# Order and shape of the first loads: q weights in four row blocks ahead of most of x

## Chip, cores and metric

The kernel runs on one core of a Trainium2 chip. The metric is the time of one execution on the device in microseconds (us). Six runs of the kernel before gave 203.6 to 205.08, median 204.03.

## What is computed

Two branches share one layer norm and are added to the input:

```python
x = A_x                                   # (1, 2048, 512), bf16
xn = layernorm(x)
# A: sliding, dilated local attention: 32 heads of 16, window of 8 positions with a step of 2
q, k, v = split(xn @ wqkv)                # wqkv: (512, 1536)
logits = q . k[pos - 2 w] / 4, w = 0..7   # positions below 0 masked
A = (softmax(logits) . v[pos - 2 w]) @ wo
# B: gated MLP with a mix over positions
z = gelu(xn @ w_in)                       # w_in: (512, 1376)
z1, z2 = z[:, :688], layernorm(z[:, 688:])
B = (z1 * (w_sp @ z2 + b_sp)) @ w_out     # w_sp: (2048, 2048)
return x + A + B
```

## The kernel before, in words

**Tiles.** The 2048 rows of x are 16 tiles of 128 rows. Tile number i = 4 tb + j: tb (0 to 3) is a block of 512 neighbouring rows, j (0 to 3) the place in it. The work goes by j: "block j" is the four tiles 4 tb + j. All of x lies in one SBUF buffer, `xall` (in the profile `r_x`), the q and k weights in `wqk` (`r_w`), each as four row blocks of 128 input channels (kc = 0 to 3, since matmuls contract over 128 at a time).

**The path of a tile.** VectorE computes statistics of its 512 columns (`ln_stats`, L205 and L206, in one part or in two halves), ScalarE the square root (`ln_sqrt`, L209), VectorE the reciprocal and the normalization (`ln_recip`, L212; `ln_apply`, L216). Then the tile is transposed into `xnT`: tiles of block 0 and the first two of block 1 by TensorE (`tr`, L223) with ScalarE copying the result out of PSUM (`tr_copy`, L227), all others by a DMA transpose on SyncE's queue (`tr_dma`, L231). After that, `qk_part` (L308) multiplies by weights: `qk_part(pq, j, m, b0, b1)` makes, for block j, two of the four column groups of q (m = 0, 1) or of k (m = 2, 3), for the tiles tb = b0 to b1 - 1, with one matmul for each column group and row block kc. `qk_copy` (L318) casts the sums to bf16 with ScalarE.

**Order.** Nothing is scheduled by a planner: each engine works through its instructions in the order in which the program writes them, and waits on semaphores where data of others are needed. After the part shown below, a written list (`ORDER`, L42) fixes the rest: the products of the MLP, v, the logits, softmax, the mix over positions (L451), the output products and the stores.

**The loads** (L171 to L180). SyncE (SP) and ScalarE (A) each issue into a DMA queue of their own; both queues are served by the same 16 DMA engines. For block 0, tiles tb = 0 and 1 come as column halves, the left one on SP, the right one on A; tiles 2 and 3 follow as one transfer of 256 KB on A. On SP behind its two halves: the q weights in one transfer of 512 KB, block 1 of x, the k weights, blocks 2 and 3 of x, and half of `w_in`. ScalarE loads its function table behind its three DMAs.

**The start of the compute** (L557 on). TensorE runs ten warm-up matmuls while the first loads come in. VectorE normalizes tiles 0 and 1 of block 0 (statistics in two halves each, as they arrive), TensorE transposes them, two more warm-up matmuls follow, then come the q products m = 0 for tiles 0 and 1 (`qk_part(pqs[0], 0, 0, 0, 2)`, split in two by row blocks). Tiles 2 and 3 are normalized and transposed; between their transposes stand the products m = 1 for tiles 0 and 1. Then:

```python
    qk_part(pqs[0], 0, 0, 2, 3)          # q, m = 0, tile 2 alone
    qk_part(pqs[1], 0, 1, 2, 3)          # q, m = 1, tile 2 alone
    qk_part(pqs[2], 0, 2, 0, 2)          # first product with the k weights
    ...
    for n in range(2):
        qk_part(pqs[n], 0, n, 3, 4)      # q, tile 3 alone
        qk_copy(pqs[n], 0, n)
```

and the rest of block 0, block 1, and the list.

Of the kernel before, what the change touches and what calls it, by code (L numbers as in the profile page):

```python
# [15 lines left out]
P = 128  # L16
S = 2048
D = 512
NT = S // P
TB = 4  # L20
TBS = 512
C = D // P
# [48 lines left out]
def kernel(  # L71
# [14 lines left out]
    A = nc.scalar  # L86
    G = nc.gpsimd
    PE = nc.tensor
    SP = nc.sync

    x2 = A_x.rearrange("b s d -> (b s) d")
    out2 = out.rearrange("b s d -> (b s) d")
    xblk = x2.rearrange("(b j p) d -> j p b d", b=TB, j=4)
# [9 lines left out]
    xall = r_x[:, 0:4 * TB * D].rearrange("p (j b d) -> p j b d", j=4, b=TB)  # L103
    vp = r_x[:].rearrange("p (d t) -> p d t", d=DH)
    r_w = sb.tile([P, 8192], BF16, name="r_w")
    wqk = r_w[:, 0:4096].rearrange("p (s k f) -> p s k f", s=2, k=C)
# [54 lines left out]
    k_casts = [[] for _ in range(4)]  # L161
    k_reads = [[] for _ in range(4)]

    def load_x0(E, tb, h):
        E.dma_start(xall[:, 0, tb, 256 * h:256 * h + 256], x2[tb * TBS:tb * TBS + P, 256 * h:256 * h + 256])  # L165

    def load_wqk(E, s):
        E.dma_start(wqk[:, s],
                    A_wqkv[:, s * D:(s + 1) * D].rearrange("(k p) f -> p k f", p=P))

    for tb in range(2):  # L171
        load_x0(SP, tb, 0)
        load_x0(A, tb, 1)
    A.dma_start(xall[:, 0, 2:4, :], xblk[0][:, 2:4, :])
    load_wqk(SP, 0)
    SP.dma_start(xall[:, 1], xblk[1])
    load_wqk(SP, 1)
    for j in range(2, 4):
        SP.dma_start(xall[:, j], xblk[j])
# [21 lines left out]
    def ln_stats(i, parts=1):  # L201
        j, tb = i % 4, i // 4
        w = D // parts
        for h in range(parts):
            V.bn_stats(stats[:, i, 6 * h:6 * h + 6], xall[:, j, tb, w * h:w * h + w])  # L205
        V.bn_aggr(mv[:, i, :], stats[:, i, 0:6 * parts])  # L206

    def ln_sqrt(sl):
        A.activation(rstd[:, sl], mv[:, sl, 1], ACT.Sqrt, bias=eps_t[:])  # L209
# [92 lines left out]
    def qk_part(pq, j, m, b0, b1, ccs=(0, 1), p0=None, kcs=range(C)):  # L302
        sd, c0 = m // 2, 2 * (m % 2)
        p0 = b0 if p0 is None else p0
        xv = xnT[:].rearrange("p k (b j t) -> p k b j t", b=TB, j=4)
        for cc in ccs:
            for kc in kcs:
                PE.matmul(pq[:, cc, p0 * P:(p0 + b1 - b0) * P], wqk[:, sd, kc, c0 + cc:D:C],  # L308
                          xv[:, kc, b0:b1, j, :], start=(kc == 0), stop=(kc == C - 1))

    def qk_copy(pq, j, m, b0=0, b1=TB, p0=None):
        sd, c0 = m // 2, 2 * (m % 2)
        p0 = b0 if p0 is None else p0
        if sd == 0:
            dst = qs[:, j, c0:c0 + 2, b0 * P:b1 * P].rearrange("p c (b t) -> p c b t", b=b1 - b0)
        else:
            dst = ks[:, c0:c0 + 2, HALO:HALO + S].rearrange("p c (b j t) -> p c b j t", b=TB, j=4)[:, :, b0:b1, j, :]
        cast = A.copy(dst, pq[:, :, p0 * P:(p0 + b1 - b0) * P].rearrange("p c (b t) -> p c b t", b=b1 - b0))  # L318
        if sd == 1:
            for i in k_reads[j]:  # L320
                tc.declare_no_dep(cast.ins, i, reason="other token columns of the same rows")
            k_casts[j].append(cast.ins)

    def qk_tile():
        return ps_mm.tile([P, 2, TBS], F32, name="pq", tag="mm")
# [213 lines left out]
    def blk(j):  # L539
        return [4 * tb + j for tb in range(TB)]  # L540

    def col(i):
        return slice(i, i + 1)
# [13 lines left out]
    t0, i1 = blk(0), blk(1)  # L557
    i2, i3 = blk(2), blk(3)
    warm_up(10)
    for n in range(2):  # L560
        ln_stats(t0[n], 2)
        ln_sqrt(col(t0[n]))
    for n in range(2):
        ln_tile(t0[n])
# [11 lines left out]
    pqs = [qk_tile() for _ in range(3)]  # L576
# [3 lines left out]
    qk_part(pqs[1], 0, 1, 0, 2, (0,))  # L580
    tr_copy(t0[3], tr(t0[3]))
    qk_part(pqs[1], 0, 1, 0, 2, (1,))
    qk_part(pqs[0], 0, 0, 2, 3)
    qk_part(pqs[1], 0, 1, 2, 3)
    qk_part(pqs[2], 0, 2, 0, 2)
    for n in range(2):
        ln_stats(i1[n])
# [4 lines left out]
    ln_apply(i1[1])  # L592
    ln_stats(i1[3])
    for n in range(2):
        qk_part(pqs[n], 0, n, 3, 4)
        qk_copy(pqs[n], 0, n)
    ln_sqrt(slice(9, 16, 4))
    ln_stats(i2[0])
# [22 lines left out]
    pqs = [qk_tile() for _ in range(3)]  # L621
# [79 lines left out]
```

## Time and profile before

| what | value |
|---|---|
| median of six runs | 204.03 us |
| the profiled execution | 204.22 us |
| its span (first to last instruction) | 202.5 us |
| TensorE busy | 196.3 us, 97% of the span |
| VectorE busy | 187.1 us, 92% |
| ScalarE busy | 100.1 us, 49% |
| granted TensorE clock | 1.00 in all slices |
| DMA moved | 25.91 MB, 128 GB/s on the mean |

Start of the kernel in the timeline (us from the start of the span):

| engine | what | from | length |
|---|---|---|---|
| SP and A | two x halves each, issue | 0.81 | 0.87 and 0.90 |
| SP | q weights, issue | 1.73 | 0.43 |
| A | x tiles 2 and 3, issue | 1.74 | 0.46 |
| A | function table load | 2.22 | 1.28 |
| VectorE | statistics of tile 0, of tile 1 | 2.86, 3.78 | 0.75, 0.70 |
| TensorE | transposes of tiles 0 and 1 | 5.25, 5.77 | |
| TensorE | first q products | 7.17 | 1.06 |
| VectorE | statistics of tile 2, of tile 3 | 6.60, 7.42 | 0.69, 0.66 |
| TensorE | transposes of tile 2, of tile 3 | 8.86, 9.53 | 0.40, 0.39 |
| TensorE | 48 matmuls of 128 or 256 columns | 9.75 | 3.70 |
| VectorE | statistics of block 1 begin | 9.23 | |
| SP | first DMA transpose | 15.40 | 1.29 |

How to read the views that follow. The *chain of work* is followed back from the last instruction, at each step to what released it. A *wait* is idle time of an engine just before an instruction, with what ended it. In the table by stretches, each engine has its busy time and the number of its instructions, and the last three columns are the granted TensorE clock, the mean busy share of the 16 DMA engines (over 1 where packets overlap) and GB/s moved. PE is TensorE's matmul, PEld its weight load, DVE VectorE, ACT ScalarE, POOL GpSimd. Matmuls are pipelined, so the time from one start to the next says more than the duration of one.

### The profile page before, as it was taken

To read this page: it belongs to the slowest core of one execution; us is meant where nothing else is said; L and a number is where in the kernel's file an instruction comes from. 1 tells how busy PE (TensorE), PEld (TensorE's weight loads), DVE (VectorE), ACT (ScalarE), POOL (GpSimd) and SP (SyncE) were. 2 spreads that over 40 slices of the span, in tenths; PEclk is the share of its full clock that TensorE was granted. 3 is DMA by queue.
4 is the path that set the end of the run, shared out by engine and by line. 5 is a ranking of instruction groups with operands and counts; after the bars stand their busy time and mean duration, and the time that the engine had idled before them with its cause. 6 is when DMAs were issued, how large, how long until landed. Compare 5 with 4: busy or idle time off the path is not lost.

```text
span 202.5 us, 4070 instructions
## 1 busy us (share of the span) xinstructions
PE 196.3 (97%) x1687; PEld 124.6 (62%) x1691; DVE 187.1 (92%) x267; ACT 100.1 (49%) x162; POOL 11.7 (6%) x14
## 2 busy tenths in 40 slices
PE   7799999999999999999999999999999999999994
PEld 2599856555566666666556666666546645664562
DVE  5789899999999999999989998999999999999805
ACT  3466999999969984641742309647100210031000
POOL 3000000792000000000000000000000000000000
PEclk9999999999999999999999999999999999999999
DMA  5972558000397000695499966989717910744164
GB/s 149 359 256 53 104 103 238 10 0 3 71 181 165 3 0 0 120 258 114 33 231 206 177 163 105 207 166 189 163 40 195 212 43 0 223 95 94 51 200 136
DMA packets 66290, 25.91 MB, mean 128 GB/s; under 512 B 56224, under 2 KB 66016, under 8 KB 66016
## 3 DMA queue, kind: packets, MB, share of 16 engines
q1 hardware_dynamic: 65568, 25.19, 53.6%
q10 hardware_dynamic: 704, 0.47, 0.7%
q8 instruction: 13, 0.21, 0.4%
q14 instruction: 5, 0.04, 0.1%
HBM read 10.13 MB, written 2.10 MB: 60 GB/s over the span
## 4 chain that ended last, share of the span: by engine, by line
PE 93%; DMA 2%; DVE 2%; issue 1%; ACTq 0%; DVEq 0%
PE pg L451 37%; PE pz L237 19%; PE pq L308 13%; PE po L523 7%; PE pv L412 7%; PE po L499 6%; DMA r_x<-in_A_x_dram 2%; PE pl L362 1%; DVE r_qk L513 1%; PE po L508 1%; PE pb L499 1%; DVE stats L205 1%; PE pt L223 1%; PE pa L308 0%; ACTq L165 0%
## 5 line engine op out<-in xcount | busy, mean ns | idle before, releaser
L451 PE MATMUL pg<-z,r_qk 128*128 128x344 bf16 x448 | 67.3, 309 | 0.0
L451 PEld LDWEIGHTS <-r_qk 128*128 128x128 bf16 x448 | 43.7, 98 | 22.4 <-issue 0.8
L237 PE MATMUL pz<-w_z,xnT 128*128 128x344 bf16 x256 | 40.1, 309 | 0.0
L426 DVE TENSOR_TENSOR r_pr<-r_x,r_w 128x2048 bf16<-128x2048 bf16 x32 | 38.2, 1218 | 0.3
L430 DVE TENSOR_TENSOR r_pr<-r_pr 128x2048 bf16<-128x2048 bf16 x28 | 33.9, 1218 | 0.2
L457 ACT ACTIVATE gs<-pg,b_col 128x688 bf16<-128x688 f32 x16 | 13.3, 831 | 40.7 <-PE pg L451 25.1
L237 PEld LDWEIGHTS <-xnT 128*128 128x128 bf16 x256 | 24.9, 98 | 13.4 <-issue 0.8
L308 PE MATMUL pq<-xnT,r_w 128*128 128x256 bf16 (+2 forms) x192 | 28.8, 304 | 0.7 <-DMA r_w<-in_A_wqkv_dram 0.7
L342 DVE TENSOR_TENSOR r_pr<-r_qk 128x2048 bf16<-128x2048 bf16 x24 | 28.4, 1216 | 0.0
L308 PEld LDWEIGHTS <-r_w 128*128 128x128 bf16 x200 | 20.2, 114 | 7.8 <-DMA r_w<-in_A_wqkv_dram 1.1
L299 ACT ACTIVATE r_uz<-pz 128x688 bf16<-128x688 f32 x16 | 11.4, 741 | 22.5 <-PE pz L237 22.3
L318 ACT CAST r_qk<-pq 128x1024 bf16<-128x1024 f32 (+1 forms) x16 | 15.3, 990 | 2.4 <-PE pq L308 2.3
L523 PE MATMUL po<-r_w,r_uz 128*128 128x512 bf16 x66 | 14.9, 379 | 0.6 <-issue 0.6
L513 DVE TENSOR_TENSOR r_qk<-po,r_qk 128x512 bf16<-128x512 f32 x14 | 9.2, 686 | 6.0 <-PE po L523 6.0
L412 PE MATMUL pv<-xnT,r_w 128*32 128x512 bf16 x256 | 14.6, 380 | 0.0
L499 PE MATMUL po<-r_lg,r_pr 32*128 32x512 bf16 x224 | 14.5, 375 | 0.0
L523 PEld LDWEIGHTS <-r_uz 128*128 128x128 bf16 x85 | 8.0, 98 | 9.8 <-issue 1.5
L351 DVE TENSOR_TENSOR r_pr<-r_pr 128x4096 bf16<-128x4096 bf16 x6 | 13.7, 2283 | 0.0
L205 DVE BATCH_NORM_STATS2 stats<-r_x 128x6 f32<-128x512 bf16 (+1 forms) x18 | 10.8, 611 | 1.9 <-DMA r_x<-in_A_x_dram 1.9
L261 ACT ACTIVATE junk<-z 128x688 bf16<-128x688 bf16 x16 | 12.4, 778 | 0.2
L412 PEld LDWEIGHTS <-r_w 128*32 128x32 bf16 x256 | 9.4, 138 | 4.6 <-issue 0.3
L255 ACT ACTIVATE z<-pz 128x688 bf16<-128x688 f32 x16 | 11.8, 738 | 0.8 <-PE pz L237 0.8
(81 smaller groups left out, 175.1 us busy)
## 6 DMA issues: line engine op xcount, KB each, us to landing
r_lg<-in_A_wo_dram SPq DMA_DIRECT2D x8, 256.0 KB, 3.9
r_qk<-in_A_x_dram SPq DMA_DIRECT2D x16, 128.0 KB, 2.2
out_dram<-r_qk SPq DMA_DIRECT2D x15, 128.0 KB, 1.9
r_w<-in_A_wqkv_dram SPq DMA_DIRECT2D x3, 512.0 KB, 5.0
r_x<-in_A_x_dram SPq DMA_DIRECT2D x3, 512.0 KB, 6.4
w_z<-in_B_w_in_dram SPq DMA_DIRECT2D x2, 688.0 KB, 5.7
r_w<-in_B_w_out_dram SPq DMA_DIRECT2D x1, 640.0 KB, 4.8
r_x<-in_A_x_dram ACTq DMA_DIRECT2D x1, 256.0 KB, 4.8
```

The source lines that it names most:

```text
L237: PE.matmul(pz[:, hh, 0:FHALF], xnT[:, kc, i * P:(i + 1) * P], wz[:, kc, hh * FHALF:(hh + 1) * FHALF], start=(kc == 0), stop=(kc == C - 1))
L308: PE.matmul(pq[:, cc, p0 * P:(p0 + b1 - b0) * P], wqk[:, sd, kc, c0 + cc:D:C], xv[:, kc, b0:b1, j, :], start=(kc == 0), stop=(kc == C - 1))
L318: cast = A.copy(dst, pq[:, :, p0 * P:(p0 + b1 - b0) * P].rearrange("p c (b t) -> p c b t", b=b1 - b0))
L342: prod = V.tensor_tensor(pr[g % 3][:, c].rearrange("p w b t -> p b w t"), q3.unsqueeze(2).broadcast_to([P, TB, 4, P]), k4, ALU.mult)
L351: V.tensor_tensor(pr[g % 3][:, 0:2], pr[g % 3][:, 0:2], pr[g % 3][:, 2:4], ALU.add)
L412: PE.matmul(pv[32 * tb:32 * tb + 32, dd, :], wv[:, kc, 2 * d2 + dd, :], xnT[:, kc, tb * TBS:(tb + 1) * TBS], start=(kc == 0), stop=(kc == ...
L426: V.tensor_tensor(pw_t[n], vp[:, :, off:off + P], a_sb[:, slot_w(w), ts].unsqueeze(1).broadcast_to([P, DH, P]), ALU.mult)
L430: V.tensor_tensor(pw_t[n] if dst is None else dst, pw_t[n], pw_t[m], ALU.add)
L451: PE.matmul(pg[:, hh, 0:FHALF], wsp[n][:, k, :], z2[:, k, hh * FHALF:(hh + 1) * FHALF], start=(k == 0), stop=(k == NT - 1))
L457: A.activation(gs[:], tiles.pop(("g", n))[:, :, 0:FHALF], ACT.Identity, bias=b_col[:, i:i + 1])
L499: PE.matmul(pc, op[32 * tb:32 * tb + 32, d, o * P:(o + 1) * P], wo_r[32 * tb:32 * tb + 32, d, cs], start=(d == 8), stop=False, tile_positi ...
L523: PE.matmul(pc, uT[:, o % 2, m, tb * P:(tb + 1) * P], wout[:, m, cs], start=False, stop=(m == MCH - 3))
```

## The change

The left and right column halves remain for tile 0 only; tiles 1, 2 and 3 are each loaded whole on ScalarE's queue. SP issues its half of tile 0, then the q weights as four transfers of 128 input channels each, then what it issued before. The statistics of tile 1 are taken in one part. The q products for tile 2 alone and tile 3 alone become one call for both, at the place where tile 3's stood, so that the first product with the k weights moves ahead of them.

```diff
-    def load_x0(E, tb, h):
-        E.dma_start(xall[:, 0, tb, 256 * h:256 * h + 256], x2[tb * TBS:tb * TBS + P, 256 * h:256 * h + 256])
-
-    def load_wqk(E, s):
-        E.dma_start(wqk[:, s],
-                    A_wqkv[:, s * D:(s + 1) * D].rearrange("(k p) f -> p k f", p=P))
-
-    for tb in range(2):
-        load_x0(SP, tb, 0)
-        load_x0(A, tb, 1)
-    A.dma_start(xall[:, 0, 2:4, :], xblk[0][:, 2:4, :])
-    load_wqk(SP, 0)
+    def load_x0(E, tb, c0=0, c1=D):
+        E.dma_start(xall[:, 0, tb, c0:c1], x2[tb * TBS:tb * TBS + P, c0:c1])
+
+    def load_wqk(E, s, k0=0, k1=C):
+        E.dma_start(wqk[:, s, k0:k1],
+                    A_wqkv[:, s * D:(s + 1) * D].rearrange("(k p) f -> p k f", p=P)[:, k0:k1])
+
+    load_x0(SP, 0, 0, D // 2)
+    load_x0(A, 0, D // 2, D)
+    for tb in range(1, TB):
+        load_x0(A, tb)
+    for k in range(C):
+        load_wqk(SP, 0, k, k + 1)
     SP.dma_start(xall[:, 1], xblk[1])
     load_wqk(SP, 1)
...
     for n in range(2):
-        ln_stats(t0[n], 2)
+        ln_stats(t0[n], 2 - n)
         ln_sqrt(col(t0[n]))
...
     qk_part(pqs[1], 0, 1, 0, 2, (1,))
-    qk_part(pqs[0], 0, 0, 2, 3)
-    qk_part(pqs[1], 0, 1, 2, 3)
     qk_part(pqs[2], 0, 2, 0, 2)
...
     for n in range(2):
-        qk_part(pqs[n], 0, n, 3, 4)
+        qk_part(pqs[n], 0, n, 2, 4)
         qk_copy(pqs[n], 0, n)
```

## The prediction

> **What bounds the kernel now.** I read the page's chain of work first, then TensorE's waits, then the chain of the first 12 us, then the DMA traffic of those microseconds.
>
> ```profile
> PE 93%; DMA 2%; DVE 2%; issue 1%; ACTq 0%; DVEq 0%
> ```
>
> The chain that ended last is TensorE for 93% of the span. The 2% of DMA is one transfer at the start. The waits of TensorE over the whole span say the same:
>
> ```profile
> PE pwm L550 <- DVE warm L183: 1.1, 1, 1.1
> PE pq L308 <- DMA r_w<-in_A_wqkv_dram: 0.7, 1, 0.7
> PE po L523 <- issue: 0.6, 4, 0.2
> PE pt L223 <- DVE r_x L216: 0.6, 1, 0.6
> ```
>
> Columns: us in total, times, longest. After its start TensorE waits twice (0.68 us for the q weights at 7.17, 0.62 us for normalized x tile 2 at 8.86) and then never again by more than 0.16 us until the tail. So a microsecond won or lost before about 13 us arrives at the end one for one, as nothing behind it can absorb it or add to it. The chain through the second wait (start, length):
>
> ```profile
> 1.74 4.84 DMA r_x<-in_A_x_dram
> 6.58 0.02 issue
> 6.60 0.70 DVE stats L205
> ...
> 8.38 0.42 DVE r_x L216
> 8.81 0.05 issue
> 8.86 0.40 PE pt L223 x4
> ```
>
> x tiles 2 and 3 are one 256 KB transfer that lands 4.84 us after its issue; only then VectorE starts on them. VectorE had been idle since 5.71, so 0.89 us. Why the transfer is slow shows in a table by stretches (last two columns: DMA share, GB/s):
>
> ```profile
> 1.75:2.75 1.00, 1.00 (x4) 0.30 (x3) 0.07 (x1) 0.53 (x1) 0.81 (x4) 1.00 0.75 218
> 2.75:3.75 1.00, 1.00 (x4) 0.44 (x3) 0.85 (x3) 0.76 (x1) 0.00 (x0) 1.00 0.59 102
> 3.75:4.75 1.00, 1.00 (x4) 0.29 (x2) 0.96 (x5) 0.29 (x1) 0.00 (x0) 1.00 0.99 324
> 4.75:6.75 2.00, 1.56 (x12) 0.56 (x10) 1.05 (x4) 1.36 (x4) 0.00 (x0) 1.00 1.07 370
> 6.75:12.75 6.00, 4.96 (x63) 4.68 (x64) 5.72 (x18) 2.31 (x7) 0.00 (x0) 1.00 1.09 354
> ```
>
> There is a **trough**: the four small x transfers are through by about 3.0, and the next two (the 512 KB of q weights, the 256 KB of x), though issued at 1.73 and 1.74, hardly move before 3.75. That microsecond carries 0.10 MB where the later rate would carry 0.35 MB; 0.25 MB at 354 GB/s is **0.71 us lost**. From 3.75 on the DMA engines are full, so everything queued behind is late by it: the second x block (issue 2.20, 6.4 us to landing, so 8.6) and the k weights (512 KB more, 0.524/0.35 = 1.5 us later, so 10.1).
>
> **The change, part by part.**
>
> *Column halves of tile 1 and the pair of tiles 2 and 3 become three whole tiles on ScalarE's queue.* ScalarE issues four DMAs instead of three, 0.45 us each (rows of 0.40 to 0.47). Behind them in its queue stands the table load: 2.22 becomes 2.67, its 1.28 us end at 3.95. The first square root, now at 3.89, slips by 0.06; VectorE wants its result at 4.63, and the instruction takes 0.29, so 0.4 us of cover stays and I cost it at 0. Beyond that cover each 0.1 us would cost 0.1.
>
> *Statistics of tile 1 in one part.* Two halves took 0.70, one whole row of 512 takes 0.69 (tile 2's row): 0. But they now need all of tile 1 at 3.78, and the first tile's apply stands behind them on VectorE. Loads of this form (128 KB, one row per partition) exist in the trace, the residual x loads: 2.2 us to landing. From an issue at 1.24 that is 3.4, the lower bound. With what goes ahead of it (0.13 MB of 512-byte packets, then 0.26 MB at 354 GB/s, from 1.75) its last byte moves at about 2.9; the last of the 16 engines lands 0.5 to 0.8 behind (the old pair: some 5.9 by the same count, landed 6.58), so 3.4 to 3.7. If the whole trough falls ahead of it, 4.1 to 4.4, 0.3 to 0.6 too late. I take 3.7, nearest to the 2.2 us row: no cost.
>
> *Tiles 2 and 3.* By the same count tile 2 lands at 4.2 to 4.5, tile 3 (0.92 MB into the stream) at 4.9 to 5.2; even with the full trough under 6. Upper bound, the old 4.84 us from an issue at 2.2: 7.0. VectorE gets to them at 5.71 and 6.53. So VectorE's 0.89 us of idle go, and the chain to the transposes moves up whole: tile 2's from 8.86 to 7.97, tile 3's from 9.53 to 8.64. What is late next is VectorE itself, which is then without a gap: **0.89 us is the cap** of this part.
>
> *q weights in four row blocks.* SP issues 1 + 4 instead of 2 + 1 transfers ahead of the second x block. The build gives the fourth block a wait on the landing of tile 0's ScalarE half (3.04 now), as DMA semaphores are reused; queued behind on SP are the second x block (2.20 becomes 3.5), the k weights (2.75 becomes 4.0, behind tile 1's landing), and blocks 3 and 4 of x. As long as the rings hold data this is hidden: by 3.5 some 0.9 MB are queued, which last to 4.4. The first q products wait for blocks 0 and 1 only; with all four landed by 5.4 the limit becomes ScalarE's copies, which end at 6.85. TensorE's 0.68 us wait thus shrinks, but it then stands longer ahead of tile 2's transposes: not on the path, 0.
>
> Does the trough go? From below 0 (it only moves: a few first packets of the weights took 0.2 to 0.67 us each in the records of single packets, wherever they come), from above 0.71, plus 0.06 for tile 1's 512-byte packets (27 ns, against 46 ns for 1 KB) that double in size. I take 0.65, as the new transfers have the form of the first x halves, whose data flowed 0.6 us after the issue ended, while it was the many-row form that took 1.6. The k weights then land at 10.1 - 0.65 = 9.5.
>
> A rule speaks against the split. The row: 128 KB loads land 2.2 us after their issue one by one, and the one large transfer stands in the trough. The Trainium skill, "DMA: Bandwidth & Descriptors", section "Rules for kernel authors", wants many small transfers coalesced into one large one, and its section "Anatomy of one DMA" has about 2 us of fixed cost for each (there for the path from GpSimd). An estimate from that page, with the cost paid block after block, has the q weights 3 x 2 = 6 us later and the kernel slower by some 5; with the cost overlapped, as several transfers in flight in the trace suggest, nothing.
>
> *Two early product parts leave the front, later ones double.* 32 matmuls of 128 columns become 16 of 256. TensorE's timeline has them at 0.056 and 0.109 us apart: 1.79 against 1.745, 0.05 won. But the removed 16 (0.9 us) stood ahead of the first k product, which waits for the k weights: now it starts at 11.08, in the shade of 10.1 by a full microsecond; after the change TensorE reaches it at 8.86 + 4 x 0.109 = **9.30**. Behind it stand 8 + 16 matmuls of 256 columns, 2.62 us, up to the point reached now at 12.85. So the gain is 12.85 - 2.62 - T = **10.23 - T**, T being the later of 9.30 and the landing of the k weights.
>
> **The sum.** T = 9.5: 10.23 - 9.5 = 0.73 us, of a possible 0.93. The later stations move along: x block 2's statistics at 8.34 (landing 8.6 - 0.65 = 7.95), the DMA transposes, which wait for VectorE and ScalarE's casts (both earlier by at least this much), and from there TensorE has no gap. The profiled execution took 204.22, span 202.5 and 1.7 around it; it becomes 203.5. Median of the runs 204.03, so **203.3**.
>
> **Rivals.**
> *The trough only moves (0.22).* Slow first packets of the weights then stall the rings at 2.3 instead of 2.9, tile 1 lands at 4.1 to 4.4, the k weights at 10.1 as now. The wait for the q weights is replaced by one for the k weights, 0.84 us at the first k product. T = 10.1, gain 0.1: 203.9. For it: DMA share 0.59 at 102 GB/s, so the engines were half busy in the trough. Against: the other half they had nothing to do.
> *The SP queue falls behind (0.15).* If the second x block and the k weights keep their distance from their issues (6.4 and 7.4 us), they land at 3.5 + 6.4 = 9.9 and 4.0 + 7.4 = 11.4; TensorE stands at the first k product until then: 10.23 - 11.4 = -1.2, 205.2. It turns to a loss where the k weights land later than 10.23. Against: 354 GB/s at a share of 1.09 from 4.75 to 12.75; the bytes, not the issues, set those landings.
> *VectorE is fully relieved (in the main case's upper part).* With k weights by 9.3: gain 0.93, and 0.2 more if tile 0 lands sooner with less beside it: 202.9 to 203.1.
>
> **Chances.** Main case 0.63, of which 0.23 above 0.5% (1.02 us, about what a measurement of this kernel can tell from no change): the cap lies just under it, and medians wander by 0.3 (203.6 to 205.08 were seen). With the second case 0.22 within, the third 0.15 slower: faster 0.23, same 0.62, slower 0.15. The range goes from the cap with that wobble, 202.7, to the no-gain case with its own, 204.8; the SP case stays outside.
>
> **What will show it.** Right: over 250 GB/s between 2.75 and 3.75; VectorE's statistics of tile 2 at 5.7 without a wait; tile 2's transposes at 8.0; the first k product at 9.3 to 9.6, with a short DMA wait on the weights; no new TensorE wait after. Wrong: that trough again; a wait of over 0.5 us at the first k product; VectorE idle before tile 1's statistics; or a TensorE gap past 13 us, which this account excludes.

## The result, and the profile after

The changed kernel takes a median of **205.17 us** in 19 runs (204.23 to 207.93), the kernel before 204.08 in 38 runs beside them (203.6 to 205.26). The ratio is **1.0050, 95% interval 1.0036 to 1.0064**: 0.7 to 1.3 us slower. The run of 207.93 was a slow one (granted clock 0.992) and is left out of the ratio, not of the median. The forecast was 203.3 with a range of 202.7 to 204.8, so it was wrong in sign, and the time lies outside the range. What came is the rival "The SP queue falls behind", in its place and nearly with its price.

The profiled execution of the changed kernel took 205.82 us, span 204.1. It is 0.65 above its median, so this profile shows the effect larger than it is on the mean. The page's chain of work, to be held against PE 93% and DMA 2%:

```profile
PE 92%; DMA 5%; issue 1%; DVEq 0%; ACTq 0%; DVE 0%
```

TensorE's waits over the span (us in total, times, longest):

```profile
PE pq L309 <- DMA r_w<-in_A_wqkv_dram: 1.5, 1, 1.5
PE pwm L551 <- DVE warm L184: 1.1, 1, 1.1
PE po L524 <- issue: 0.6, 4, 0.2
PE pt L224 <- DVE r_x L217: 0.4, 2, 0.2
```

The wait for the q weights (0.7) is gone and the one for tile 2 (0.6) has shrunk to 0.2. In their place is one wait of 1.5 us, once, at the first product with the *k* weights. The chain of work over the first 16 us (start, length) says what holds those weights up:

```profile
1.23 2.97 DMA r_x<-in_A_x_dram
4.20 0.02 issue
4.22 7.07 DMA r_w<-in_A_wqkv_dram
11.29 0.05 issue
11.34 3.25 PE pq L309 x28
```

Read it upward: the product at 11.34 waits for the k weights, 7.07 us from issue to landing; their issue at 4.22 waits for x tile 1 on ScalarE's queue to land (the reused DMA semaphore). The timeline of SP and the instructions named in the prediction (start, length):

```profile
1.27 2.31 SPq L168 DMA_DIRECT2D r_w<-in_A_wqkv_dram  x4
3.62 0.43 SPq L177 DMA_DIRECT2D r_x<-in_A_x_dram  x1
4.22 0.39 SPq L168 DMA_DIRECT2D r_w<-in_A_wqkv_dram  x1
4.22 0.69 DVE L206 BATCH_NORM_STATS2 stats<-r_x 128x6 f32<-128x512 bf16 x1
6.07 0.69 DVE L206 BATCH_NORM_STATS2 stats<-r_x 128x6 f32<-128x512 bf16 x1
8.32 0.40 PE L224 MATMUL pt<-ident,r_x 128*128 128x128 bf16 x4 [0.22 <-DVE r_x L217]
```

The second x block is issued at 3.62 (2.20 before), the k weights at 4.22 (2.75 before). Tile 1's statistics begin at 4.22, not 3.78; tile 2's at 6.07 without a wait. In the table by stretches (last columns: clock, DMA share, GB/s):

```profile
1.75:2.75 1.00, 1.00 (x4) 0.31 (x3) 0.07 (x1) 0.04 (x1) 0.81 (x4) 1.00 0.65 188
2.75:3.75 1.00, 1.00 (x4) 0.45 (x3) 0.66 (x2) 1.00 (x1) 0.00 (x0) 1.00 0.86 286
3.75:4.75 1.00, 1.00 (x4) 0.31 (x3) 0.83 (x3) 0.54 (x2) 0.00 (x0) 1.00 1.00 342
4.75:6.75 2.00, 1.70 (x12) 0.65 (x11) 1.89 (x7) 0.92 (x3) 0.00 (x0) 1.00 0.91 251
6.75:12.75 6.00, 4.13 (x39) 3.43 (x38) 4.70 (x17) 2.50 (x7) 0.00 (x0) 1.00 1.07 357
```

The trough between 2.75 and 3.75 has filled: 286 GB/s instead of 102. But **a second one has opened later**: 251 GB/s instead of 370 between 4.75 and 6.75. The DMA traffic of its deepest part, 5.0 to 6.2:

```profile
DMA packets 243, 0.22 MB, mean 187 GB/s; under 512 B 24, under 2 KB 243, under 8 KB 243
q1 hardware_dynamic: 205, 0.19, 73.8%
q10 hardware_dynamic: 38, 0.03, 7.9%
```

In the first trough 0.18 MB more went through (286 - 102 in 1 us), in the second 0.20 MB less (1.2 us at 187 where 354 is the later rate). They cancel. The 16 DMA engines did not stand empty for all of that time: the packets of SP's queue (q1) and ScalarE's (q10) kept them busy for 82% of it (73.8% and 7.9%). The records of single packets show why so little moved: 18 packets of 1 KB took over 0.1 us each, 6.1 us together or 0.4 us for each engine, where most take 0.046.

Nor were all engines late. In this execution 15 of the 16 had their part of the k weights by 10.16, about when the kernel before has all of them (10.14); the last one alone came at 11.29.

**Where the time is, in sum.** In every profile of a complete kernel here but one, 185.33 us pass from block 1's first q product (the first product of 512 columns; its start is called the *front* below) to the end of the last matmul. So an execution is front + 185.33 + the end behind the last matmul + 1.7 around the span. Before: 14.17 + 185.33 + 3.01 + 1.71 = 204.22. After: 15.31 + 185.33 + 3.47 + 1.71 = 205.82. Of the 1.60 between these two executions, 1.14 is in the front and 0.46 in the end.

### The profile page after: what moved, and what is told of

It reads as the page before. It is cut to its first block, busy times and chain, and to the rows that moved or that the text cites. A ratio compares the mean times of both kernels' runs of the same rounds, so it can differ in the third digit from the quotient of the medians.

```text
span 204.1 us, 4038 instructions
## 1 busy us (share of the span) xinstructions
PE 196.8 (96%) x1671; PEld 124.7 (61%) x1675; DVE 187.1 (92%) x266; ACT 100.1 (49%) x162; POOL 11.6 (6%) x14
## 4 chain that ended last, share of the span: by engine, by line
PE 92%; DMA 5%; issue 1%; DVEq 0%; ACTq 0%; DVE 0%
PE pg L452 37%; PE pz L238 18%; PE pq L309 12%; PE po L524 7%; PE pv L413 7%; PE po L500 6%; DMA r_w<-in_A_wqkv_dram 3%; DMA r_x<-in_A_x_dram 1%; PE pl L363 1%; PE pa L524 1%; PE po L509 1%; PE pb L500 1%; PE pa L309 0%; DVEq L695 0%; PE pt L224 0%
## 5 line engine op out<-in xcount | busy, mean ns | idle before, releaser
L309 PE MATMUL pq<-xnT,r_w 128*128 128x256 bf16 (+1 forms) x176 | 28.9, 316 | 1.7 <-DMA r_w<-in_A_wqkv_dram 1.5
```

## The experiments

The theory: SP's issues come late, so the k weights land late, and they matter because the product order pulled the first k product 0.9 us forward. Rivals: the product order itself costs; whole tile 1 costs; the loss sits behind the front. Executions of one kernel differ by over 1 us, so times are compared over 12 runs, and mechanisms by each profile's own front and landings.

### One part of the change at a time

`e1_old_products`: the changed loads, the products in their old places.

```diff
     qk_part(pqs[1], 0, 1, 0, 2, (1,))
+    qk_part(pqs[0], 0, 0, 2, 3)
+    qk_part(pqs[1], 0, 1, 2, 3)
     qk_part(pqs[2], 0, 2, 0, 2)
...
-        qk_part(pqs[n], 0, n, 2, 4)
+        qk_part(pqs[n], 0, n, 3, 4)
```

> The loads of the changed kernel, with the q products of tile 2 and tile 3 in their old places (16 matmuls of 128 columns ahead of the first k product). Theory A (the k weights land some 1.2 us later because SP's later loads are issued late, and the first k product, pulled 0.9 us forward, has to wait for them): the k weights land at about 11.3 as in the changed kernel, TensorE reaches the first k product at about 10.5 and waits 0.7 to 0.8 us instead of 1.5; the point before the last k products comes at 11.34 + 0.87 + 0.89 = 13.1 against 12.85 before, so +0.25 us against the kernel before, 0.85 faster than the changed one. Theory B (the loads themselves are not the matter, the new order of the products is): the whole loss goes, 204.1 or less. Theory C (something outside the first 14 us costs, such as the later stages or the tail): stays at +1.1.

Measured: 204.46, before beside it 204.35, ratio 1.0004 (0.9981 to 1.0028). Its k weights landed as late as 10.66, and still its front is 13.82. Its chain of work:

```profile
4.10 6.56 DMA r_w<-in_A_wqkv_dram
10.66 0.05 issue
10.71 2.40 PE pq L309 x28
```

The first k product starts the moment the weights land, at 10.71, but only 3.11 us pass from there to the front; in the changed kernel it is 3.97 (11.34 to 15.31). The 16 narrow products that the change moved behind the first k product are those 0.86 us: in the old order they are done while the k weights are awaited.

`e2_old_loads`: the loads of before, the new product order.

```diff
-    qk_part(pqs[0], 0, 0, 2, 3)
-    qk_part(pqs[1], 0, 1, 2, 3)
     qk_part(pqs[2], 0, 2, 0, 2)
...
-        qk_part(pqs[n], 0, n, 3, 4)
+        qk_part(pqs[n], 0, n, 2, 4)
```

> The loads of the kernel before, with the new order of the products alone. Theory A: the first k product is reached at 11.08 - 0.90 = 10.19, just behind the k weights at about 10.1; gain 0.05 us, so within 0.2 us of the kernel before. Theory B: slower by about 1 us, as the changed kernel is.

Measured: 204.14, ratio 0.9997 (0.9978 to 1.0017). The order alone shows no cost. But it has no reserve: its chain passes through the k weights too.

```profile
2.82 6.88 DMA r_w<-in_A_wqkv_dram
9.71 0.05 issue
9.75 3.25 PE pq L308 x28
```

So neither half is slow by itself, within half a microsecond; the loss needs both.

### Fewer issues on SP

`e3_two_blocks`: the q weights in two blocks of 256 KB.

```diff
-    for k in range(C):
-        load_wqk(SP, 0, k, k + 1)
+    for k in range(0, C, 2):
+        load_wqk(SP, 0, k, k + 2)
```

> The changed kernel with the q weights in two transfers of 256 KB instead of four of 128 KB, so that SP has two transfers fewer ahead of the second x block and no semaphore is used again before the k weights. Theory A: the second x block is issued at about 2.2 instead of 3.6, the dip of DMA traffic between 4.75 and 6.75 goes (over 330 GB/s), the k weights land at 9.5 to 10.2, gain 0.0 to 0.6 us against the kernel before: 203.5 to 204.1. Theory D (the transfers beside each other, or one slow DMA engine, make the k weights late, whatever the issue times): k weights stay at about 11.3, +1 us.

`e4_pair`: x tiles 2 and 3 as one transfer again. One semaphore fewer is used, so the fourth weight block waits for nothing.

```diff
-    for tb in range(1, TB):
-        load_x0(A, tb)
+    load_x0(A, 1)
+    A.dma_start(xall[:, 0, 2:4, :], xblk[0][:, 2:4, :])
```

> The changed kernel with x tiles 2 and 3 as one pair again, one transfer fewer: the fourth block of the q weights then has no wait, and the second x block is issued at about 3.25 (behind the landing of tile 0) instead of 3.62. Theory A: a part of the loss goes, as the issue is 0.4 us earlier: k weights at 10.8 to 11.0, +0.6 to +0.8 us against the kernel before. Theory D: k weights at 11.3, +1.1.

Measured: e3 204.73, ratio 1.0015 (0.9990 to 1.0040); e4 205.01, ratio 1.0044 (1.0016 to 1.0071). With two blocks the second x block is issued at 2.24 and the second trough does not exist, as e3's table by stretches shows:

```profile
2.75:3.75 1.00, 1.00 (x4) 0.45 (x3) 0.79 (x3) 0.99 (x1) 0.00 (x0) 1.00 0.77 247
4.75:6.75 2.00, 1.07 (x6) 0.32 (x4) 1.67 (x6) 0.29 (x1) 0.00 (x0) 1.00 1.07 366
```

Its k weights land at 9.55 and nothing waits for them. What ate this gain is in the timeline of e3's profile (205.57, its slowest run): tile 1, whole and now behind larger weight blocks, lands at 4.95, and VectorE waits for it.

```profile
4.97 0.69 DVE L206 BATCH_NORM_STATS2 stats<-r_x 128x6 f32<-128x512 bf16 x1 [1.05 <-DMA r_x<-in_A_x_dram]
```

In e4 the wait falls on the second x block itself and costs next to nothing: four issues of 0.43 us stand ahead of it and end at 3.10, the landing comes at 3.14, and the block is issued at 3.15; 314 GB/s from 4.75 to 6.75, k weights at 10.16. Against the changed kernel's profile the wait is thus a third of the lateness (3.62 to 3.15), the number of issues the rest; in h1 (below), which has the changed loads with their wait, the block is issued at 3.20, so the wait's part differs between executions.

e4 also warns against reading the loss from the front alone. Its front in the profile is 14.18, as before, and still its time is 1.0044: the profiled execution, 205.18, has its excess in the end, 3.83.

### How far executions differ

`a_again1`, `a_again2` are the changed kernel, `b_again1`, `b_again2` the kernel before, without an edit.

> The changed kernel as it is, for a second profile of it: how much of the late k weights and of the longer end (3.47 us from the last matmul to the end of the span, 3.01 before) is there every time. Theory A (SP issues the second x block 1.4 us later and the rings run dry): DMA traffic between 4.75 and 6.75 again under 300 GB/s, most of the 16 engines of the k weights at 9.2 or later, TensorE waits 0.5 to 1.5 us at the first k product. Theory E (one DMA engine happened to be late in the one profile): no wait there, and the loss lies elsewhere.

> As the run before it: a third profile of the changed kernel. Theory A: a wait of 0.5 to 1.5 us at the first k product; theory E: none.

> The kernel before as it is, for a second profile of it. Theory A: no wait at the first k product, the product of 512 columns starts at 13.7 to 14.2, the end after the last matmul is 3.0 to 3.5 us, as in the other profiles. If the end is 3.4 to 3.8 in all other profiles, the 3.01 of the first profile was its low side, and the ends say nothing of the change.

> As the run before it: a third profile of the kernel before, for the spread of its front (13.7 to 14.2 expected) and of its end (3.0 to 3.8).

Measured: 204.44 and 205.14; 204.44 and 205.09. The faster execution of the changed kernel has its k weights at 9.85 instead of 11.29; its chain:

```profile
4.23 5.62 DMA r_w<-in_A_wqkv_dram
9.85 0.05 issue
9.90 3.25 PE pq L309 x28
```

TensorE shows no listed wait there, yet the chain still passes through this landing. All profiles with the new product order but e3's, where tile 1 bounds, follow the formula of the prediction (front moved = 10.23 - T; T is the start of the first k product, front before 14.17):

| kernel | k weights landed | T | 10.23 - T | front earlier by |
|---|---|---|---|---|
| after | 11.29 | 11.34 | -1.11 | -1.14 |
| f2 (below) | 10.92 | 10.97 | -0.74 | -0.77 |
| f3 (below) | 10.85 | 10.90 | -0.67 | -0.70 |
| a_again2 | 10.27 | 10.32 | -0.09 | -0.12 |
| e4 | 10.16 | 10.21 | +0.02 | -0.01 |
| f4 (below) | 10.06 | 10.11 | +0.12 | +0.09 |
| a_again1 | 9.85 | 9.90 | +0.33 | +0.30 |
| e2 | 9.71 | 9.75 | +0.48 | +0.45 |
| h1 (below) | 9.64 | 9.69 | +0.54 | +0.51 |

### The front by itself

Four cut kernels end behind the k products of block 0. Their ends differ, so their fronts are compared, not their times. `f1_front_before` is the kernel before, cut; `f2_front_changed` the changed one, cut. `f3_front_late` has the loads of before and the new product order, with three tiny loads between the q weights and the second x block, which delay SP and add 384 packets of 2 bytes:

```diff
+    tiny = sb.tile([P, 4], BF16, name="tiny")
+    for n in range(3):
+        SP.dma_start(tiny[:, n:n + 1], x2[0:P, n:n + 1])
     SP.dma_start(xall[:, 1], xblk[1])
```

`f4_front_pool` is f2 with x tile 3 and the fourth q block issued by GpSimd, so that SP has one issue less and no wait:

```diff
-        load_x0(A, tb)
+        load_x0(G if tb == 3 else A, tb)
...
-        load_wqk(SP, 0, k, k + 1)
+        load_wqk(G if k == 3 else SP, 0, k, k + 1)
```

> The kernel before, cut off behind the last k product of block 0: everything from the statistics of tiles 6, 10 and 14 on is left out, the two DMA transposes of block 1 too, and one part of the k result is stored. All loads ahead of that are there. Its time is that of the front alone, without the spread of the stores at the end. It is the base for the three cut kernels beside it; some 20 us, plus the time around the span.

> The changed kernel, cut off in the same place. Theory A (late k weights at the first k product): 0.4 to 1.1 us slower than the cut kernel before, wait at the first k product 0.5 to 1.5 us. Theory F (the front costs nothing on the mean, the loss is in the stores at the end): within 0.15 us of it.

> The loads of the kernel before with the changed order of the products and three tiny loads (128 rows of 2 bytes) on SP between the q weights and the second x block, cut off in the same place: SP issues the second x block at about 3.5 as in the changed kernel, while x and the q weights come as before. Theory A (what counts is when SP issues the later loads): the k weights land 0.4 to 1.1 us later than in the cut kernel before, and so does the front. Theory D (the small transfers of x and of the weights beside each other are what delays them): front within 0.15 us of the cut kernel before.

> The changed kernel with x tile 3 and the fourth block of the q weights issued on GpSimd's queue, so that SP issues the second x block at about 2.7 without a wait; cut off in the same place. Theory A: k weights at 9.4 to 9.8, front 0.3 to 0.6 us faster than the cut kernel before. Theory D: k weights still at 10.5 to 11.3, 0.3 to 1.1 us slower than it. If GpSimd's transfers land after 6.5, VectorE or TensorE wait for them instead, and the run says nothing on A.

| kernel | median us | profiled us | second x block issued | GB/s, 4.75 to 6.75 | k weights landed | front |
|---|---|---|---|---|---|---|
| f1 | 22.76 | 22.76 | 2.18 | 376 | 9.66 | 14.28 |
| f2 | 22.51 | 22.71 | 3.29 | 309 | 10.92 | 14.94 |
| f3 | 23.09 | 22.65 | 3.69 | 274 | 10.85 | 14.87 |
| f4 | 22.12 | 22.03 | 2.66 | 332 | 10.06 | 14.08 |

The changed front comes 0.66 us later from profile to profile (14.94, 14.28). How much of this is the mean is open: f2's profile is at the top of its six runs (22.01 to 22.71). If the spread lies in the front, the difference is 14.74 - 14.28 = **0.46 us** at f2's median, and next to nothing at its lowest runs (22.01, 22.11). The whole times do not show the loss: f2's median is below f1's, as its end behind the last matmul is 4.17 us and f1's 4.79.

f3 is the nearest to SP's lateness alone: the loads of before, issued late, and the k weights go from 9.66 to 10.85. In the seven profiles with the loads of before they land at 9.66 to 10.53, and on the half-way engine at 9.25 to 9.49; f3 has 10.85 and 9.78, outside both. A part of that is the tiny packets' own: they took 3.4 us in all, 0.2 us of each engine, between 5.6 and 6.4, and f3's DMA share there is high for what it moved:

```profile
4.75:6.75 2.00, 1.38 (x12) 0.56 (x10) 0.92 (x4) 1.34 (x4) 0.00 (x0) 1.00 1.10 274
```

Its chain of work:

```profile
3.69 0.43 SPq L179
4.12 0.04 issue
4.17 6.69 DMA r_w<-in_A_wqkv_dram
10.85 0.05 issue
10.90 1.95 PE pq L311 x16
```

Over the profiles, the later the second x block is issued, the deeper is the second trough: 357 to 376 GB/s where it is issued by 2.24 (e3 and the kernels with the loads of before), 355 to 366 at 2.71 and 2.72 (g2, h2, g3 below), 314 to 329 at 3.15 to 3.20 (e4, h1), 289 to 309 at 3.29 to 3.44 (f2, a_again), 281 at 3.54 (e1), 251 at 3.62 (after), 274 at 3.69 (f3). f4's 332 at 2.66 is out of line: g3 has the same loads.

The last step, from the trough to the last engine's landing, is looser. The k weights land at 9.43 to 10.53 in the twelve profiles where the second x block is issued by 2.72 (9.9 on the mean), and at 9.64 to 11.29 in the eight where it is issued at 3.15 or later (10.5). The means are 0.5 us apart, but the ranges overlap.

### Other ways to the same end

`g2_x_first` is the kernel before with tile 2 whole on SP ahead of the q weights and tile 3 whole on ScalarE's queue; `g3_pool_old_products` has f4's loads and the old product order.

```diff
-    A.dma_start(xall[:, 0, 2:4, :], xblk[0][:, 2:4, :])
+    for tb, E in ((2, SP), (3, A)):
+        E.dma_start(xall[:, 0, tb], xblk[0][:, tb])
     load_wqk(SP, 0)
```

> The kernel before with x tiles 2 and 3 as two whole tiles, tile 2 on SP ahead of the q weights and tile 3 on ScalarE's queue; all else as before (halves for tiles 0 and 1, q weights in one transfer, old products). Theory A: SP issues the second x block at 2.7 without a wait, so k weights land at 9.3 to 10.0, ahead of their use at 10.2; tiles 2 and 3 are there by 5.7 and 6.5, VectorE's idle 0.89 us goes, the product of 512 columns starts at 13.2 to 13.5; 0.5 to 0.9 us faster than the kernel before. Theory D (small transfers delay what is behind them): k weights at 10.5 or later, no gain. If the q weights land after 6.9, TensorE waits for them and a part of the gain goes.

> The changed loads with x tile 3 and the fourth block of the q weights on GpSimd's queue, and the products in their old places: k weights at about 10 as in the cut kernel with the same loads, the first k product reached at about 10.6, no wait. Theory A: front limited by VectorE alone (tile 1 at 4.2), product of 512 columns at 13.8 to 13.9, 0.3 us faster than the kernel before in the front; by theory G the end takes 0 to 0.4 of it, so 203.8 to 204.3. Theory D: a wait at the first k product again, +0.3 or more.

Measured: g2 204.08, ratio 0.9993 (0.9974 to 1.0013); g3 203.96, ratio 0.9987 (0.9968 to 1.0007). No version is faster clear of the noise. Yet in g2's profile (204.57, its slowest run) the front is 13.39, 0.78 earlier than before, and TensorE's waits for x and q weights have gone:

```profile
PE pwm L551 <- DVE warm L184: 1.1, 1, 1.1
PE po L524 <- issue: 0.6, 4, 0.2
PE pq L309 <- ACT xnT L228: 0.2, 1, 0.2
```

It was given back behind the last matmul: 4.14 us instead of 3.01.

### The end behind the last matmul

VectorE's waits in the last 10 us show what is longer. Before:

```profile
DVE r_qk L513 <- PE po L523: 5.4, 2, 5.0
```

After:

```profile
DVE r_qk L514 <- PE po L524: 5.8, 3, 5.0
DVE r_qk L514 <- DMA out_dram<-r_qk: 0.4, 1, 0.4
```

g2:

```profile
DVE r_qk L514 <- PE po L524: 5.4, 2, 5.0
DVE r_qk L514 <- DMA out_dram<-r_qk: 1.1, 1, 1.1
```

One of the last additions waits for an earlier store to land. On SP that store stands behind an x load whose issue takes 1.2 to 1.8 us instead of 0.43, beside a packet of 16 KB on the instruction queue that takes 0.9 to 1.5 us, in every profile of a complete kernel. The rest of the difference is in the waits that close the kernel: the landing of the last store is waited for fourth in the kernel before and second in the changed one, where three others follow at 0.06 us each (last landing to end of the span 0.90 before, 0.99 after). The change uses three DMA semaphores more at the start, so all later DMAs take them in a shifted round. Theory: the shift makes the end longer. Rival: the ends only scatter. Tiny loads behind the load of `w_z2` shift the round (`g1_shift`, `h3_before_shift3`: the kernel before, three of them) or bring it back (`h1_changed_shift5`: the changed kernel, five; `h2_x_first_shift7`: g2, seven). In the h kernels they have 16 rows; in g1 128, and three of them:

```diff
     SP.dma_start(w_z2[:], B_w_in[:, FH:F].rearrange("(k p) f -> p k f", p=P))
+    tiny = sb.tile([16, 8], BF16, name="tiny")
+    for n in range(5):
+        SP.dma_start(tiny[:, n:n + 1], x2[0:16, n:n + 1])
```

> The kernel before with three tiny loads (128 rows of 2 bytes) on SP behind the last of the early loads, where SP then stands idle for 8 us. Nothing else changes, but the later DMAs take the semaphores that they take in the changed kernel (three places on in a ring of eight). Theory G (that shift lengthens the end: the last store's semaphore is waited for second instead of fourth, and the others behind it): the end after the last matmul 0.1 us longer than 0.89 us behind the last landing, 3.35 to 3.8 us in all, +0.1 to +0.4 us against the kernel before; front as before (13.7 to 14.7). Theory H (the longer ends of the changed kernels are chance, or come from the new early loads in some other way): end 3.0 to 3.4, within 0.1 us of the kernel before.

> The changed kernel with five tiny loads (16 rows of 2 bytes) on SP behind the last early load, so that all later DMAs take the same semaphores as in the kernel before. Theory G (the shift of the semaphores lengthens the end): end after the last matmul back to 3.0 to 3.4 us, the last landing 0.89 ahead of the end of the span, and the loss shrinks to what the front costs, +0.3 to +0.7 us. Theory H: end 3.45 to 3.8, +1.0 us as the changed kernel.

> The kernel with x tiles 2 and 3 whole and tile 2 ahead of the q weights (front 0.8 us faster in its profile), with seven such tiny loads, so that the later DMAs take the semaphores of the kernel before. Theory G: end 3.0 to 3.4, and the front's gain comes through: 0.6 to 0.9 us faster than the kernel before. Theory H: end 3.45 to 4.1 as without them, 0.1 to 0.4 us faster.

> The kernel before with three such tiny loads, the shift of the changed kernel alone, for a second profile of its end. Theory G: end 3.45 to 3.8, 0.99 us from the last landing to the end of the span, +0.1 to +0.4 us. Theory H: end 3.0 to 3.4, +0.0.

| kernel | median us, ratio (95%) | end in the profile | last landing to end |
|---|---|---|---|
| g1 | 204.34, 1.0012 (0.9987 to 1.0037) | 3.62 | 1.00 |
| h3 | 204.31, 1.0003 (0.9988 to 1.0018) | 3.42 | 0.99 |
| h1 | 204.99, 1.0030 (1.0015 to 1.0045) | 3.05 | 0.90 |
| h2 | 205.35, 1.0038 (1.0014 to 1.0062) | 3.60 | 1.07 |

For the theory: the end is 3.01 to 3.40 in the four profiles with the round of before (before, b_again1 and 2, e2) and 3.05 in h1, which has it back; it is 3.42 to 4.14 in ten others of complete kernels, whose round is shifted. Against it: h2 has the round back as well, and its end is 3.60; and the shift alone does not move the times of g1 and h3 by an amount that can be told from nothing. h1 stands at 1.0030 where the changed kernel stands at 1.0050, with intervals that overlap. (h2's time tells nothing of the end: its seven loads delay the DMA transposes on SP, TensorE waits 1.0 us for one, and 186.51 us pass from the front to the last matmul.) The 0.1 us of the closing waits fits the theory, but for h2: 0.89 or 0.90 in those four and h1, 0.99 or 1.00 in the six that are shifted by three (after, a_again1 and 2, e1, g1, h3), and 1.07 in h2, which should have 0.90.

The larger part is the wait of that addition, and over the 16 profiles of complete kernels it follows the long issue of the x load: 0.04 to 0.46 us where that issue took 1.22 to 1.46 us (before, b_again1 and 2, e2, h1, h2, h3), 0.41 to 1.06 where it took 1.47 to 1.84 (the other nine). The six profiles with the round of before all stand on the short side, of the ten with a shifted round h3 alone. In the kernel before the issue took 1.26 to 1.40, in the changed one 1.50 to 1.83, and the wait is some 0.3 us longer there. Why that issue would take longer in a shifted round stays **open**.

## Why the prediction was wrong

**What bounds the kernel: right, but for the end.** "A microsecond won or lost before about 13 us arrives at the end one for one": 185.33 us behind the front in both kernels, and no TensorE gap past 13 us. What the step left out is the end behind the last matmul, on which the chain lies as well: 3.01, 3.25 and 3.32 in three executions of the kernel before, 3.47, 3.54 and 3.81 in three of the changed kernel.

**"As long as the rings hold data this is hidden: by 3.5 some 0.9 MB are queued, which last to 4.4": the step that failed.** The count compared the *issue* of the second x block (3.5 forecast, 3.62 measured) with the end of the queued data, as if data flowed from the issue on. But that block is of the same many-row form as the load in the old trough, and the next paragraph of the prediction held that this form took 1.6 us. 3.6 + 1.6 is 5.2, behind the 4.4 at which the queue was said to be empty; the second trough lies at 5.0 to 6.2. The number was in the text and was applied to one transfer only. f3 shows the lateness (k weights 9.66 to 10.85, a part of it the tiny packets), e3 the other side (issue at 2.24: no second trough). So the lateness was not hidden: the second trough stands in all eight profiles in which the second x block is issued at 3.15 or later. That it is an emptied queue, as this count would have it, is only a part: the engines were busy for 82% of its deepest stretch, and 18 packets took 0.1 to 0.7 us each instead of 0.046. Why they did stays open.

**"T = 9.5", the term of the sum.** It measured 11.34, 9.90 and 10.32 in three executions, and 9.69 to 10.97 in h1 and f2, which have the same loads. The formula 10.23 - T held within 0.03 us in nine profiles; T alone was wrong. Two things make it late. Half of the 16 DMA engines have the k weights at 9.22 on the mean of six profiles with these loads (after, a_again1 and 2, e1, f2, h1), 9.36 on the mean of seven with the loads of before: for the typical engine the trough has only moved, which is the rival "The trough only moves". But the last engine lands at 10.44 on the mean (9.64 to 11.29), against 10.01 (9.66 to 10.53), and the product waits for the last. What makes the last engine lag more (2.07 us behind the half-way engine in the changed kernel's profile, 0.70 in a_again1) was not settled. In the profiled execution it is the whole loss in front: with the fifteenth engine's 10.16 for the last one's 11.29, the formula gives 0.0. (The statistics of the second x block, put at 8.34, began at 9.80 behind its late landing; TensorE did not wait for them.)

**"The SP queue falls behind": place right, price right by luck.** It said k weights at 11.4, second x block at 9.9, time 205.2; measured 11.29, 9.78, and a median of 205.17. Its reason, a fixed distance from the issue, does not hold: the x block took 6.16 us in one execution and 4.65 in another. And only a part of its price is the front, 0.2 to 0.7 us by the estimates below. Its time came out by a second cause, the end.

**How the loss divides is an estimate.** The whole loss is 1.02 us (0.73 to 1.31). The end is longer by 0.4 on the mean of the profiles (3.61 in three of the changed kernel; 3.25 in four with the round of before). What remains for the front is 0.7, by subtraction alone. The cut kernels give it 0.46 at their medians, and the profiles 0.2: the fronts are 14.41 on the mean of five with the changed loads and order (13.66 to 15.31; after, a_again1 and 2, f2, h1) and 14.22 of six with those of before (13.50 to 14.65; before, b_again1 and 2, f1, g1, h3). That a part of the loss is the front, and needs both the late k weights and the product order, rests on the times: e1 and e2 have one half each and show no loss, with intervals that do not meet the changed kernel's.

**Statistics of tile 1 in one part: "3.4 to 3.7 ... no cost" failed.** It lands at 4.20, what the text gave for the case in which the whole trough falls ahead of it (4.1 to 4.4). In eight further profiles with four weight blocks its statistics begin between 4.04 and 4.26. VectorE loses 0.44 at 3.78 (in this profile tile 0's statistics, too, begin 0.23 later, at 3.09, so not all of it is tile 1's), and of its cap of 0.89 about half is left: tile 2's transposes come 0.54 earlier (8.86 to 8.32), not 0.89. The first k product could be reached at about 9.7, not 9.30, and the most that this front could win was 0.5, not 0.93.

**ScalarE's fourth issue, at 0: right.** The table load ends at 3.99 (3.95 forecast), and the first square root at 4.13 follows tile 0's later statistics.

**Merged products, at about 0: right as a cost** (e2: 0.9997), wrong in what was not asked. The order was read as a gain with a cap. It is also a loss of reserve, 0.86 us of work that used to stand between q and k.

**The Trainium skill**, "DMA: Bandwidth & Descriptors", "Rules for kernel authors", wants small transfers coalesced: the four blocks landed at 3.97, 5.19, 5.67 and 6.86, where the one transfer landed at 7.12, so nothing like the 6 us of the prediction's estimate, which had the fixed cost of "Anatomy of one DMA" paid block after block. The direction was right all the same, by another cost: each further transfer holds SP for some 0.46 us (e4's four issues take 1.83). "Rules for kernel authors" also says that spreading transfers over issuing engines gives no bandwidth and only saves issue time of the sequencer. f4 and g3 agree in that the issue time is saved: two transfers on GpSimd brought the second x block from 3.29 (f2) to 2.66 and 2.72. The rate from 4.75 to 6.75 rose from 309 GB/s to 332 and 366.

## What to carry to other kernels

When a transfer is split on a queue, count the issue time of what stands behind it, add the time that this transfer's form needs until its data flow (the trace has it), and compare that sum with the time at which the queued bytes run out. Before work is moved away from ahead of a wait, ask what that work was covering: a reorder that costs nothing can still make a transfer critical that was not. When a gain at the front does not arrive, look behind the last matmul as well, and compare several executions of each kernel: of three profiles of the changed kernel one had its front 1.14 us late, one 0.12 late and one 0.30 early.

## What the runs showed of the hardware

- A load of 512 KB spreads over 16 DMA engines that finish apart: the k weights had landed on half of them at 9.22, on 15 at 10.16 and on the last at 11.29 in one execution, at 9.15 and 9.85 in another of the same kernel.
- The first 512 KB transfer on SP left a dip in both kernels, in another place: at 2.75 to 3.75 (102 GB/s) where it was the q weights, at 5.0 to 6.2 (187 GB/s) where it was the second x block, issued late. Where the second x block was issued by 2.24, 357 to 376 GB/s moved from 4.75 to 6.75. In the later dip the DMA engines were busy for 82% of the time: 18 packets of 1 KB took over 0.1 us each, where most took 0.046.
- An issue on SP that takes 0.43 us elsewhere took 1.2 to 1.8 us some 6 us before the last matmul's end, beside a 16 KB packet on the instruction queue. A store is issued behind it, and the addition that waits for this store waited 0.04 to 0.46 us where the issue took up to 1.46, and 0.41 to 1.06 where it took more.
